# Projections and some MLP passes as two 64-row halves at once, in new engine orders

## The chip, the core and the metric

The kernel runs on one core of a Trainium2 chip. The core has TensorE (PE, the matrix engine, whose weight loads the profile shows apart as PEld), VectorE (DVE), ScalarE (ACT), GpSimd (POOL) and SyncE (SP), which here issues most of the transfers. All five run their own instruction queues in order and wait for each other on semaphores. The metric is the time of one execution on the device in microseconds; lower is better. A time below is a median over runs of one kernel, and the profile is of one execution.

## The reference

With x of 2048 rows and 448 columns (D), the result is a gated sum of two branches:

```
g = sigmoid(x @ gate_w)                      # one gate per row
a = memory_attention(x) @ wo                 # 16 heads of 28, 4 segments of 512 rows
h = layernorm(x)                              # per row
b = (gelu(h.T @ w1 + b1) @ w2 + b2).T         # mixes across the 2048 rows
out = g * a + (1 - g) * b
```

In the attention branch q, k and v are x times a 448x448 matrix each. Within a segment each head does causal softmax attention. It also reads a memory M (28x28) and z (28) that earlier segments have left: `phi(q) M / (phi(q) z + 1e-6)`, with `phi(t) = t + 1` where t > 0, and `exp(t)` elsewhere. Each head mixes the two by `sigmoid(beta)`; then M grows by `phi(k)^T v` and z by the column sums of `phi(k)`. In the other branch the normalised rows are mixed across rows: 2048 to 1792 columns by w1, a bias and a tanh gelu, and back by w2 with a bias.

Both branches read the same x, and all inputs are bf16.

## The kernel before, in words

**How it is put together.** `build_kernel` describes the work as named operations (`op`), each with an engine, a function that emits its instructions, and the tiles it reads and writes. `Sched.plan` then takes the order of each engine's queue from a table of names, `ORDER`, written out in full: `u1-0@6*5` means the operations `u1-0` to `u1-4` in a row, the first of them taking PSUM bank 6. `finalize` gives each operation the semaphore waits it needs. Nothing else sets the order: what stands earlier in an engine's list runs earlier, and waits if it must.

**The names on PE.** `warm` is nine matmuls without use, to keep the array busy at the start; `gtr` turns the gate weights, and DVE's `gw` copies the result into a 449th column of the v weights; `btr` turns the biases. `pr...` and `lo...` are the projections: `t` for v (one per 128 rows, `prt0` to `prt15`), `k` and `q` for one block of 512 rows (0 to 3) and one group of four heads, `x` for a group that holds leftover heads of both k and q. `sc` fills four banks with scores, ACT's `exp` empties them, POOL's `mask` cuts the triangle, `pv` is the product with v, `mem` and `mst` belong to the memory, `wo` and `lw` are the output projection, `u` the first MLP product (14 sums of 16 passes), `y` the second (16 sums of 14; the last in two parts of 320 and 128 columns, the second part named `y15-k#1`).

**The contraction of 448.** 448 is three chunks of 128 and a half. The x chunks start at rows 0, 128, 256 and 320, so that chunk 3 repeats half of chunk 2. `pair(A, B)` computes two projections together, each into its own bank: three full passes of 128 rows each, and one operation `lo` in which A's last 64 rows and B's run as two matmuls in the upper and the lower half of the array. That makes seven passes for two projections. `wo_pair` does likewise for the output projection (`lw` is the shared pass). For the first four v tiles and the first k projections the first chunks are separate operations, `pra` and `prb`.

**Forms of the array.** A matmul uses the array whole, or as row tiles of 64 (`lo`, `lw`) or 32 rows (`sc`), or as column tiles of 32 (`pv`, `mst`), or both (`mem`). `plan` looks at each run of PE operations between row-tiled ones; where a column-tiled one stands in the run, all full passes in it are emitted as four 32-column ones (`mm`, line 282), so that the form does not change within a run.

**Early loads.** On ACT's queue stand, in this order, the loads of v weights chunk 0, gate weights, v weights chunks 1, 2, and the last, then the last k chunk and the biases. On SP's queue stand the two transposing loads of the first 512 rows of x (chunks 0 to 2, chunk 3), k and q weights, then the next rows. DVE copies the k and q weights into a padded layout (`padk`, `padx`, `padq`, line 662) before k and q can run. Normalisation of x for the MLP is DVE work: statistics `bns` (line 916), `bna`, and `ln` (line 932), with a power on POOL in between; `u` passes of row tile t need `ln` of t.

## Time and profile before

| what | value |
|---|---|
| time, median of 3 runs | 170.95 us (170.28 to 175.36) |
| span of the profiled execution, first to last instruction | 168.9 us |
| profiled execution's own time, taken as | 168.9 us, and the 2.05 us by which the median stands above it |
| PE busy | 164.7 us (98%), 2022 matmuls recorded |
| DVE busy | 136.7 us (81%) |
| ACT busy | 130.6 us (77%) |
| POOL busy | 64.3 us (38%) |
| scores, exponential of one fill on ACT | 1.88 us, 40 of them |

How to read the profile: a group of instructions is told by line, engine, operation and tile shape, with its count, its busy time, the mean length of one in ns, and the idle time of the engine before it with what ended that. Most matmuls have line 282, that of the helper `mm`, so shapes tell them apart. A matmul's recorded length holds the time its last columns need to leave the array, so that the lengths of matmuls in a row overlap; the distance of their starts is the pace. The timeline merges like instructions in a row into one line: start, length, work and count. In it a `q` behind an engine's name (ACTq, SPq) means its sequencer, which issues transfers.

### The profile page before, as it was taken

The page shows a single profiled execution, that of the slowest core. Times are in us where ns is not written, and L with a number is a line of the kernel's source. Part 1 is how long each engine was busy: PE and PEld are TensorE (multiplying, and loading weights), DVE is VectorE, ACT ScalarE, POOL GpSimd, SP SyncE. Part 2 cuts the span into 40 slices and gives each one's busy share as a digit, 9 for nine tenths or more (in the row PEclk, how much of TensorE's full clock was granted, in tenths as well). Part 3 has the DMA queues.
Part 4 walks back from the last instruction along what each step waited for, and adds up shares of the span by engine and source line. Part 5 has one row for each costly group of instructions (what it writes and reads, how often), then busy time and mean ns, then how long its engine had stood idle before and what let it go on. Part 6 is the DMA issues. An engine that isn't in the chain of part 4 may idle for free.

```text
span 168.9 us, 4944 instructions
## 1 busy us (share of the span) xinstructions
PE 164.7 (98%) x2022; PEld 78.5 (47%) x2026; DVE 136.7 (81%) x321; ACT 130.6 (77%) x164; POOL 64.3 (38%) x100
## 2 busy tenths in 40 slices
PE   8999999999999999999999999999999999999994
PEld 2334444444554644544453454444454444564553
DVE  0088999877989989999999999999999978695042
ACT  0359999999999997999999998988985788604100
POOL 5000245260442524142177356445837355540000
PEclk9999999999999999999999999999999999999999
DMA  6998999888699945994337302328853129831202
GB/s 144 249 258 289 248 153 246 160 228 226 138 167 254 222 101 146 163 213 124 109 98 169 82 4 65 94 82 111 244 148 110 46 70 280 229 103 60 84 27 82
DMA packets 53974, 25.44 MB, mean 151 GB/s; under 512 B 18416, under 2 KB 53712, under 8 KB 53952
## 3 DMA queue, kind: packets, MB, share of 16 engines
q1 hardware_dynamic: 53160, 24.54, 61.2%
q10 hardware_dynamic: 792, 0.58, 1.7%
q8 instruction: 16, 0.26, 0.7%
q14 instruction: 6, 0.05, 0.1%
HBM read 18.82 MB, written 2.36 MB: 125 GB/s over the span
## 4 chain that ended last, share of the span: by engine, by line
PE 94%; DMA 3%; ACTq 1%; issue 1%; POOL 0%; DVE 0%; POOLq 0%
PE t L282 79%; PE t L973 8%; PE t L1003 5%; DMA t<-in_A_wv_dram 3%; PE t L856 1%; PE t L1076 1%; ACTq L525 1%; ACTq L546 0%; DVE t L1165 0%; POOL t L544 0%; POOL t L620 0%; POOL t L587 0%; POOL t L619 0%; POOL t L615 0%; POOLq L1280 0%
## 5 line engine op out<-in xcount | busy, mean ns | idle before, releaser
L282 PE MATMUL t<-t 128*32 128x448 bf16 (+9 forms) x1257 | 140.4, 352 | 1.0 <-issue 0.6
L282 PEld LDWEIGHTS t<-t 128*32 128x32 bf16 (+2 forms) x1261 | 63.7, 97 | 63.8 <-issue 15.3
L982 ACT ACTIVATE t<-t 128x2048 bf16<-128x2048 f32 x40 | 75.2, 1879 | 6.8 <-PE t L973 6.2
L985 POOL TENSOR_SCALAR_AFFINE_SELECT t<-t 128x512 bf16<-128x512 bf16 x64 | 43.3, 688 | 43.0 <-ACT t L982 40.0
L1040 POOL TENSOR_TENSOR t<-t 128x448 bf16<-128x448 f32 (+2 forms) x13 | 13.3, 1026 | 19.0 <-DVE t L1033 14.4
L1165 DVE SCALAR_TENSOR_TENSOR t<-t 128x448 bf16<-128x448 f32 (+2 forms) x17 | 10.7, 642 | 10.6 <-PE t L282 10.5
L973 PE MATMUL t<-t 28*128 28x512 bf16 (+3 forms) x256 | 15.8, 301 | 0.0
L1017 DVE STREAM_TRANSPOSE t<-t 128x512 f32<-128x512 f32 x16 | 11.3, 706 | 2.9 <-PE t L1003 2.7
L925 POOL TENSOR_TENSOR t<-t 128x4 f32<-128x4 f32 x4 | 4.2, 1054 | 23.4 <-DVE t L923 21.4
L1119 ACT ACTIVATE t<-t 128x448 bf16<-128x448 f32 x10 | 7.1, 732 | 7.6 <-PE t L282 7.6
L1003 PE MATMUL t<-t 128*32 128x512 bf16 (+3 forms) x256 | 11.5, 300 | 0.0
L1059 DVE STREAM_TRANSPOSE t<-t 128x512 bf16<-128x512 bf16 x16 | 10.9, 690 | 0.0
L973 PEld LDWEIGHTS t<-t 28*128 28x128 bf16 x256 | 4.4, 92 | 14.0 <-ACT t L982 7.7
L818 ACT ACTIVATE t<-t 128x448 bf16<-128x448 f32 x13 | 6.8, 546 | 4.2 <-PE t L282 4.2
L916 DVE BATCH_NORM_STATS2 t<-t 128x6 f32<-128x448 bf16 x16 | 9.3, 610 | 0.7 <-DMA t<-in_A_x_dram 0.7
L1145 DVE SCALAR_TENSOR_TENSOR t<-t 128x448 f32<-128x448 f32 x14 | 9.0, 649 | 0.7 <-ACT t L1140 0.6
L1003 PEld LDWEIGHTS t<-t 128*32 128x32 bf16 x256 | 6.7, 96 | 5.3 <-issue 0.7
L1137 ACT ACTIVATE t<-t 128x448 f32<-128x448 f32 x14 | 8.8, 638 | 0.1
L779 ACT ACTIVATE t<-t 128x512 bf16<-128x512 bf16 x12 | 7.6, 635 | 1.4 <-DVE t L736 1.4
L808 DVE SCALAR_TENSOR_TENSOR t<-t 128x512 bf16<-128x512 bf16 x12 | 8.5, 712 | 0.1
L1143 DVE TENSOR_SCALAR t<-t 128x448 f32<-128x448 f32 x10 | 6.5, 676 | 2.4 <-ACT t L1137 2.3
L1033 DVE SCALAR_TENSOR_TENSOR t<-t 128x448 f32<-128x448 f32 x12 | 8.4, 699 | 0.0
(76 smaller groups left out, 132.1 us busy)
## 6 DMA issues: line engine op xcount, KB each, us to landing
t<-in_B_w_dram SPq DMA_DIRECT2D x52, 256.0 KB, 3.9
t<-in_A_x_dram SPq DMA_DIRECT2D x4, 448.0 KB, 5.4
out_dram<-t SPq DMA_DIRECT2D x15, 112.0 KB, 2.0
t<-in_B_w_dram SPq DMA_DIRECT2D x8, 128.0 KB, 2.5
t<-in_A_wv_dram ACTq DMA_DIRECT2D x4, 112.0 KB, 4.1
t<-in_A_wq_dram SPq DMA_DIRECT2D x1, 336.0 KB, 4.8
spare_heads<-t SPq DMA_DIRECT2D x8, 32.0 KB
spare_heads<-t SPq DMA_DIRECT2D x16, 16.0 KB
```

Of the source, the lines that this page charges most:

```text
L282: last = e.matmul(out[q], w[:, q], x, skip_group_check=True, **kw)
L916: op("DVE", lambda e: e.bn_stats(st6[:, t, :], xh[:, t, :]), reads=[R_x[t]], writes=[R_st6[t]], name=f"bns{t}", cost=512, prio=P_PROJ - 10 ...
L973: last = e.matmul(bank(hl)[:, c0 : c0 + w], kT[r, hg, s * 512 + j * 128 : s * 512 + j * 128 + 128], qT[r, hg, s * 512 + 128 * j : s * 512 ...
L982: op("ACT", lambda e: e.activation(pslot(g), ps[:, 0:4, :], ACT.Exp, scale=SCALE), reads=R_bank[0:4], writes=[g.res], take=g, name=f"exp{p ...
L985: op("POOL", lambda e, c0=c0: e.affine_select(pslot(g)[:, :, c0 : c0 + 128], pslot(g)[:, :, c0 : c0 + 128], pattern=[[0, 4], [1, 128]], co ...
L1003: last = e.matmul(bank(cb)[32 * ((hl + hg) % 4) : 32 * ((hl + hg) % 4) + 32, 128 * j : 512], vaug[:, 4 * s + j, 32 * h : 32 * h + 32], psl ...
L1017: dv(lambda e: e.transpose(tt[:, ia, :], bank(cb)[:, 0:512]), [bres(cb)], [R_tt[ia]], "ta", 630, use=(cb,))
L1040: return e.tensor_tensor(dst, part(n3[0]), part(n3[1]), op=ALU.add)
L1059: dv(lambda e: e.transpose(oT[:, hg, s * 512 : s * 512 + 512], o), [R_ob[hg]] + ([R_obx] if hg else []), qres(hg, s), "ot", 635)
L1137: op("ACT", lambda e: e.activation(gg[:, q, :], bank(b)[:, 0:D], ACT.Square, bias=b1s[:, ft : ft + 1], scale=math.sqrt(GC)), **buse(b), re ...
L1145: op("DVE", lambda e: e.scalar_tensor_tensor(gg[:, q, :], gg[:, q, :], 1.0, vh[:, q, :], op0=ALU.add, op1=ALU.mult), reads=[R_gg[q], R_vh[ ...
L1165: op("DVE", lambda e: e.scalar_tensor_tensor(outst[:, p, c0:c1], bank(b)[:, 0 : c1 - c0], omg[:, T : T + 1], ag(T)[:, c0:c1], op0=ALU.mult ...
```

## The change: more pairs as half passes, and all five orders new

`pair` gets a second way, `halves`, used when the PE order asks for it by names (`dt0-0` to `dt0-6` in place of `lot0`, `prt0`, `prt1` and so on). The seven passes of a pair then are seven operations of two 64-row matmuls each: in each, A works on one half of the rows and B on the other half, into their two banks. In the first four A has the upper rows of the array's tile list (rows 0 to 63) and B the others, in the last three it is the other way round. Each operation waits only for the chunk that it reads (`by`). The output projection gets the same (`dw`), and pairs of MLP passes may be split alike (`u10x-2` and `u10y-2`: first one half for one sum with the other half for the other sum, then the halves change sides).

A half pass that writes a bank in which the other 64 rows wrote last now waits for that earlier operation on PE's own semaphore (`rows`, `wrote`). `btr` uses 64 rows instead of 128. The y sums no longer wait for all gelu results at their first pass, only each pass for its own. All five orders are new; 116 passes are in half form by the new names (v tiles 0 to 5, 10 and 11; k of blocks 0 and 2 in part; q of block 0 and the split third group of block 1; output tiles 6, 7, 10, 11; five row tiles of `u10`/`u11`, nine of `u12`/`u13`, two of `y8`/`y9`), of which the old form had 12 already as `lo` or `lw`. ACT's early loads are reordered, and some copies out of PSUM move between ACT and DVE.

```
+        wrote = {}
+        for o in self.per_eng["PE"]:
+            for b, k in o.rows:
+                mine = wrote.setdefault(b.bank if isinstance(b, Bank) else b, {})
+                o.deps = o.deps + ([mine[1 - k]] if 1 - k in mine else [])
+                mine[k] = o
...
+    def twice(name, sides, needs, bs, take, n, prio, tops, **kw):
+
+        def fn(e):
+            for (w, x), b, sm in zip(sides, bs, take):
+                last = mm(e, bank(b)[:, 0:n], w, x, **sm.flags())
+            return last
...
+    def halves(A, B, bs, prio):
+        sums = [Sum(7), Sum(7)]
+        for i, sides in enumerate((((0, 0), (0, 1)), ((1, 0), (1, 1)), ((2, 0), (2, 1)), ((3, 0), (3, 1)), ((0, 1), (0, 0)),
+                                   ((1, 1), (1, 0)), ((3, 1), (2, 0)))):
+            rows = [slice(64 * k, 64 * k + 64) for c, k in sides]
+            twice(f"d{A['name'][2:]}-{i}", [(P["w"](c, r), P["x"](c, r)) for P, (c, k), r in zip((A, B), sides, rows)],
+                  [r for P, (c, k) in zip((A, B), sides) for r in P["by"](c)], bs, sums, A["n"], prio, [k for c, k in sides],
+                  use=A["use"])
+        for P, b in zip((A, B), bs):
+            P["out"](b)
...
+                 by=lambda c: [rx[c // 3], R_wv[c], R_gw],
...
+    def both(stem, first, n, nk, bs, w, x, need, prio):
+        twin = [k for k in range(nk) if f"{stem}{first}x-{k}" in asked]
+        sums = [Sum(nk + len(twin)) for _ in bs]
+        for k in range(nk):
+            if k in twin:
+                for xy in range(2):
+                    rows = [slice(64 * h, 64 * h + 64) for h in (xy, 1 - xy)]
+                    twice(f"{stem}{first}{'xy'[xy]}-{k}", [(w(i, k, r), x(k, r)) for i, r in enumerate(rows)], need(k), bs, sums,
+                          n, prio, (xy, 1 - xy))
+                continue
...
 ORDER = {
     "PE": """
-warm gtr@4 warm2 pra0@7 pra1@4 pra2@5 pra3@6 prb3 prb2 prb0 prb1 lot2 lot0 prt1 prt3 prt2 prt0 pra0_1 pra0_2 pra0_0
-btr@7 lok0_0 lok0_2 prk0_0 prx0_3 prk0_2 prk0_1 prt7@4 prx1_3@5 prk1_2@6 lot6@7 lok1_2 loq0_0 loq0_2 prq0_2 prq0_0
...
+warm gtr@4 warm2 dt0-5@56 dt2-5@74 dt0-1 dt2-2 dt2-1 dt0-2 dt0-0 dt2-6 dt2-4 dt0-3 dt2-0 dt2-3 dt0-6 dk0_0-0*4 dt0-4
+dk0_0-4 dk0_2-0*2 dk0_0-5 dk0_2-2*2 dk0_0-6 dk0_2-4*2 lot6@67 lok1_2@45 dk0_2-6 prt6 prt7 prx1_3 prk1_2 prq1_1@6
+prq1_0@7 dq0_2-0*2 loq1_0 dq1_2-3@54 dq1_2-1 dq0_2-2 dq1_2-0 dq1_2-2 dq0_0-0 dq1_2-5 btr@6 dq0_0-1 dq1_2-6 dq0_0-2
...
     "ACT": """
-ldwv0 ldgw ldwv1 ldwv2 ldwvb ldwkb ldb1 ldb2 cpv2 cpv0 gt0 gt2 cpv1 gt3 gt1 ek0_0 cpk0_1 cpk0_3 cpq0_3 ek0_1 cpv7
...
+ldwvb ldwv2 ldwv1 ldwv0 ldgw ldwkb cpv3 cpv1 ldb1 gt1 gt2 gt3 ldb2 gt0 cpk0_2 cpv6 cpq0_3 cpv7 gt6 gt7 cpk1_3 cpq1_3
```

More of the change, by code (lines that the diff above doesn't have):

```diff
@@ L44 @@
                  "cost", "lat", "prio", "mode", "start", "end", "pos", "nbytes", "alts", "rel", "port", "take",
-                 "free", "hold", "tile", "cols")
+                 "free", "hold", "tile", "cols", "rows")
 class Sum:
@@ L706, in pair @@
            take=bs if isinstance(bs[0], Bank) and "first" not in A else None, name="lo" + A["name"][2:], mode="h",
-           cost=pe_cost(max(A["n"], B["n"])) + 4, prio=prio, hold=wait, adds=free)
+           cost=pe_cost(max(A["n"], B["n"])) + 4, prio=prio, hold=wait, adds=free, rows=((bs[0], 1), (bs[1], 0)))
         for (P, b, cs, c, rows), sm in zip(parts, sums):
@@ L1225, in build_kernel @@
     do_mst(2)
-    mlp = [(mm1, ft) for ft in range(NFT)] + [(mm2, T) for T in range(NT - 1)] + [(mm2_last, NT - 1)]
     for u in range(16):
```

269 lines of the change are left out of this document (161 added, 108 removed).

## The prediction

> **What bounds the kernel now.** The page was read first: busy shares and the chain of waits.
>
> ```profile
> span 168.9 us, 4944 instructions
> ...
> PE 164.7 (98%) x2022; PEld 78.5 (47%) x2026; DVE 136.7 (81%) x321; ACT 130.6 (77%) x164; POOL 64.3 (38%) x100
> ...
> PE 94%; DMA 3%; ACTq 1%; issue 1%; POOL 0%; DVE 0%; POOLq 0%
> ```
>
> TensorE (PE) carries 94% of the chain. Then the busy times by stage (columns: stretch, its length, busy time and count of PE, of the weight loads PEld, of DVE, ACT, POOL, then clock, DMA share, GB/s):
>
> ```profile
> 8.95:20.70 11.75, 11.70 (x67) 5.28 (x68) 10.43 (x32) 10.11 (x27) 1.04 (x1) 1.00 1.03 260
> 20.70:104.20 83.50, 82.87 (x1113) 39.48 (x1116) 77.07 (x193) 80.54 (x104) 34.93 (x49) 1.00 0.70 153
> 104.20:146.20 42.00, 42.00 (x593) 19.50 (x596) 37.70 (x75) 35.25 (x30) 22.53 (x31) 1.00 0.54 139
> ```
>
> From 8.95 us on PE has next to no gap, so a microsecond taken off PE's queue, or added to it, comes out at the end. The exceptions are in PE's timeline at the start (start, length, work; idle time and its releaser in brackets):
>
> ```profile
> 0.82 4.00 PE L651 MATMUL t<-const-bfloat16-1.0 128*128 128x512 bf16 x9 [0.82 <-PEq L1280]
> 4.62 0.21 PE L839 MATMUL t<-t 128*128 128x3 bf16 x1
> ...
> 5.21 2.02 PE L282 MATMUL t<-t 128*128 128x449 bf16 x8
> 7.52 2.90 PE L282 MATMUL t<-t 64*128 64x449 bf16 x14 [0.29 <-DMA t<-in_A_wv_dram]
> ...
> 23.51 0.40 PE L973 MATMUL t<-t 28*128 28x384 bf16 x8
> 24.16 2.64 PE L282 MATMUL t<-t 128*128 128x512 bf16 x13 [0.26 <-issue]
> ```
>
> Warm-up to 4.6; `gtr` (L839, which turns the gate weights) at 4.62; the first eight v passes at 5.21; a wait for the v weights before 7.52. The k projection's first pass starts at 8.95 (where I cut the stages). PE waits once more before 24.16.
>
> **The change, part by part.** The array's work does not change: a pair had six full passes and one pass of two 64-row halves, and has seven passes of two halves. By my count in the two orders 104 full passes become half pairs, while 128-row columns streamed stay the same in sum. What can change is the cost of a pass, the changes of tile form, waits, and when the stream starts.
>
> *A pass of two halves.* Before has some in a row:
>
> ```profile
> 14.17 0.58 PE L282 MATMUL t<-t 64*128 64x449 bf16 x4
> ...
> 14.37 0.59 PE L282 MATMUL t<-t 64*128 64x512 bf16 x4
> ...
> 14.59 0.49 PE L282 MATMUL t<-t 64*128 64x512 bf16 x4
> ```
>
> Their starts are 0.20 and 0.22 us apart (these are three answers for short windows), each for two matmuls, of 449 and 512 columns: the two halves run at once, at 0.43 ns a column, as the full passes below do (0.19 for 448). So 104 passes cost 0. The page "TensorE: Matmul & The Clock Gate" of the Trainium skill (part 3, what overlaps) speaks against the change: a weight load overlaps running matmuls only where the row group differs, and in a run of half pairs both row groups are always busy. What it would make of the time stands as a rival, worked out from a row.
>
> *Changes of tile form.* Around two score groups, late in the kernel (PE, then ACT):
>
> ```profile
> 118.81 0.39 PE L973 MATMUL t<-t 28*128 28x512 bf16 x4
> 119.14 2.07 PE L282 MATMUL t<-t 128*128 128x448 bf16 x10
> 121.19 0.40 PE L973 MATMUL t<-t 28*128 28x384 bf16 x8
> ...
> 119.26 1.88 ACT L982 ACTIVATE t<-t 128x2048 bf16<-128x2048 f32 x1
> 121.03 0.72 ACT L1119 ACTIVATE t<-t 128x448 bf16<-128x448 f32 x1
> 121.64 1.88 ACT L982 ACTIVATE t<-t 128x2048 bf16<-128x2048 f32 x1
> ```
>
> The first score group streams 512 columns (0.22 us at the pace of the half pairs) and the next form starts 0.33 us after it: a change of form costs 0.11. Counting forms (full, 64-row, 32-column, scores, memory) along the two orders gives 114 changes before and 106 after, of which 2 and 1 lie ahead of the first k pass: 7 fewer behind it, 7 x 0.11 = **-0.77 us**. A change costs the same in each kind, so I give it no wider bounds than 0.09 to 0.13 (-0.6 to -0.9).
>
> *Score groups that wait for the exponential.* The same rows: ten passes of 0.19 and one change are 2.00 us, but 119.14 to 121.19 is 2.05. The exponential ended at 121.14 (119.26 + 1.88) and the scores, which overwrite its banks, started 0.05 later. From score to score that loop takes 0.45 + 1.88 + 0.05 = 2.38 us. In the old order, between fill 3 of pair 4 and the last fill, six stretches hold only ten full passes (2.33) and wait 0.05 each, and one waits 0.06 for ACT; in the new one the shortest holds 2.44. **-0.36 us**, at best -0.4, at worst 0 (if ACT slips).
>
> *Self waits.* New: a half pass that writes a bank with the other 64 rows than the pass before waits on PE's own semaphore. Behind the waiting instruction PE's whole queue stands, and all evacuations of those banks.
>
> ```profile
> L282 PE MATMUL t<-t 128*128 128x448 bf16 x319 | 66.1, 353 | 0.0
> L282 PE MATMUL t<-t 128*32 128x448 bf16 x652 | 35.9, 353 | 0.0
> L282 PEld LDWEIGHTS t<-t 64*128 64x128 bf16 x64 | 2.6, 93 | 7.2 <-issue 4.5 <-DMA t<-in_A_x_dram 0.7 <-ACT t L821 0.5
> ```
>
> A pass of 448 is recorded 0.353 long but frees the array after 0.19, so it completes about 0.16 after its columns. In the new order eight half passes have just one other pass between themselves and the one they wait for (`dt0-1`, `dt2-0`, `dk0_0-4`, `dk0_2-4`, `dq1_2-5`, `dt4-0`, `dk2_2-4`, `u10y-10`); all others have two or more and 0.2 us to spare. Each of the eight waits 0.16 + 0.05 (the hop seen above) - 0.19 = 0.03 to 0.04. Bounds: 0, and a whole change of form, 0.11. Six lie behind the first k pass: **+0.24** (0 to +0.66).
>
> *32-column passes.* 181 before, 224 after by count. Busy time a pass is 35.9 / 163 = 0.220 against 66.1 / 319 = 0.207; the difference is the tail that closes each short run. I take 0; as an upper bound 43 x 0.013 = +0.6.
>
> *The start.* All v weights' loads and the small gate load stand on ACT's queue, and the change reorders it: the gate load moves from second place to fifth.
>
> ```profile
> 0.79 0.38 ACTq L525 DMA_DIRECT2D t<-in_A_wv_dram  x1
> 1.21 0.75 ACTq L546 DMA_DIRECT2D t<-in_gate_w_dram  x1
> 1.99 0.94 ACTq L525 DMA_DIRECT2D t<-in_A_wv_dram  x2
> 2.96 0.60 ACTq L529 DMA_DIRECT2D t<-in_A_wv_dram  x1
> ...
> t<-in_A_wv_dram ACTq DMA_DIRECT2D x4, 112.0 KB, 4.1
> ```
>
> Every v pass reads the gate column, which `gtr` and one DVE copy make from that load: 4.62 to 5.21, 0.59 us. The load's issue moves from 1.21 to 0.79 + 0.38 + 0.94 + 0.60, about 2.75, behind 448 KB on its own queue. Bounds: it lands before the warm-up ends (4.6), or as late as the last v piece did (7.4, just ahead of 7.52). With the 4.1 us of the wv loads it would be 6.85; the queue no longer stands still for the 0.75 us issue, so I take **6.5**. First v pass then at 7.1. Thirteen of the fourteen v passes come before the first k pass (13 x 0.19, and two self waits): 9.64. On the other side the k passes cannot start before the padded weights:
>
> ```profile
> 8.43 0.47 DVE L662 COPY t<-t 128x784 bf16<-128x784 bf16 x2 [3.36 <-DMA t<-in_A_wk_dram]
> ...
> 9.34 0.81 DVE L662 COPY t<-t 128x392 bf16<-128x392 bf16 x6
> ```
>
> These free the first k pass at 8.9, in both kernels. So the k stage starts 9.64 - 8.95 = 0.69 later, with one v pass (0.19) still to do: **+0.88 us** (+0.19 if the gate load lands by 5.8, +1.8 if at 7.4). The old wait before 7.52 saves nothing, the padding hid it.
>
> *The wait before 24.16.* From 23.51 the scores stream 512 columns (0.22) and one change (0.11) follows; 0.32 is left over, which the row puts to no releaser. The old order runs `prk2_1` there, which needs both parts of the third x transpose. The new one starts that stage with chunks of the first part and reaches the second part 0.7 us later: **-0.32** (0 at worst).
>
> *Other moves, each at nothing.* `btr` takes 64 rows, with no change of form around it. Evacuations that go from ACT to DVE or back are hidden while PE has a filled queue; cover gone, they cost what the DVE rival says. The SP queue's order after 24 us (W1 pieces, gathers, WO) is moved past by a few places; loads land 2.5 to 5 us after issue, and the order of the u passes has moved with them. At the end twelve y passes of 128 columns stand behind the last 320-column one instead of fourteen:
>
> ```profile
> 163.75 2.76 PE L282 MATMUL t<-t 128*128 128x448 bf16 x27
> ...
> 165.77 0.55 DVE L1165 SCALAR_TENSOR_TENSOR t<-t 128x320 bf16<-128x320 f32 x1 [0.95 <-PE t L282]
> 166.55 0.35 DVE L1165 SCALAR_TENSOR_TENSOR t<-t 128x128 bf16<-128x128 f32 x1 [0.23 <-PE t L282]
> ```
>
> DVE has 0.23 to spare before its last piece, and the two passes fewer (0.06 each) use half of it: the end stays 0.35 behind PE's. `ag14` and `ag15` now run on DVE ahead of `fin14`:
>
> ```profile
> L1123 DVE TENSOR_SCALAR t<-t 128x448 bf16<-128x448 f32 x6 | 4.4, 733 | 0.6 <-PE t L282 0.5
> ```
>
> From `wo15` to the last 320-column pass PE has seven of those, two full and two short y passes, 1.5 us by their columns, and DVE one `ag` and one `fin` (0.73 + 0.68): just covered; without the cover, about 0.1 us.
>
> **Sum.** 0.88 - 0.77 + 0.24 - 0.36 - 0.32 = -0.33 us. The profiled execution: 168.9 - 0.33 = 168.57. The median of the runs shown, 170.95, is 2.05 above that span (launch and end, untouched): 168.57 + 2.05 = **170.6 us**.
>
> **Rivals.**
> *A, the gate load is early.* The gate load is only 1.5 KB; if it slips through by 5.8, the k stage starts on the pads as before: 0.69 less. With self waits at 0 another 0.24: 170.6 - 0.9 = 169.7. For it: on the old queue it was in by the end of the warm-up. Against it: 448 KB ahead on the same queue.
>
> *B, slower: the late gate load leaves the array cold.* Nine warm-up passes take 4.00 us, 0.43 each, twice the 0.22 of a 512-column pass. The eight passes from 5.21 take 2.02, less the last one's 0.16 tail 1.86, where 8 x 0.19 is 1.51: about two of them ran at half pace, so the array came to full speed at about 5.9, with PE busy throughout. In the new order PE has nothing from 4.6 to 6.5. If the full pace then comes only after a new busy stretch, the thirteen v passes go at 0.38: 13 x 0.19 = +2.5, 173.1 us; with the load at 7.4, 174.0. It decides once the gate load lands after the warm-up and before the array has been granted full speed. The same page (part 1) has the clock rise after a busy window of about 3.4 us and fall after an idle one as long: by that rule a gap of 1.9 us costs nothing once the clock is up, and it would be up or not by where the free-running window lies; the 5.9 here agrees with a rise in the second window.
>
> *C, DVE is late with the normalised x.*
>
> ```profile
> L916 DVE BATCH_NORM_STATS2 t<-t 128x6 f32<-128x448 bf16 x16 | 9.3, 610 | 0.7 <-DMA t<-in_A_x_dram 0.7
> ...
> L932 DVE TENSOR_SCALAR t<-t 128x448 bf16<-128x448 bf16 x16 | 5.6, 389 | 0.0
> ```
>
> The new order starts the first MLP passes out of row order; `u0-9` is the eleventh. Ahead of its x tile DVE has, after the three k copies (ending at about 14.9), 15 statistics (8.7), 8 normalisations (2.8) and some 3.3 of aggregates, copies and small work (my estimate): 14.9 + 14.8 = 29.7. PE reaches `u0-9` at 29.8 by my count. A DVE chain 10% longer would hold PE 1.5 us, of which little comes back: 172.1.
>
> *D, weight loads show, or halves don't overlap.* By the skill's rule above each added pass would expose a load: 104 x 0.093 (the 64x128 row) = +9.7, 180.3 us. The starts 0.20 and 0.22 apart with two loads each say no.
>
> **How the numbers follow.** Forecast as summed 0.60; A 0.16; B 0.13; C 0.08; D 0.02; something not seen 0.01. The forecast's own range is 169.9 (gate load by 5.8) to 171.9 (load at 7.4, self waits 0.1 each). Leaving out the dear half of B, of C and all of D, and the best of A, the range is 169.3 to 173.0. A measurement of this kernel tells about 2% from no change, 167.5 and 174.4 us: nothing summed here reaches 167.5 (0.03); above 174.4 lie D and the joint ends of B and C (0.06); within, 0.91.
>
> **What would show it.** `gtr` in PE's timeline should start near 6.5 (A: 4.6; B: v passes 0.38 apart), the first 64-row 512 pass near 9.6, with its predecessors 0.19 apart; runs of half pairs at 0.19 and 0.215; no PE gap before the first MLP passes (C: gaps released by L932); scores 2.44 or more apart late on. The prediction is wrong if half pairs are spaced by more than 0.25, if PE's stream from the first k pass is not about 1.2 us shorter than before (157.6 us from 8.95 to PE's end at 166.5), or if PE shows gaps in the middle.

## The result, and the profile after

The changed kernel takes **179.17 us** (median of 4 runs, 177.98 to 179.71), the kernel before 170.75 beside it: a ratio of 1.049 (95% interval 1.044 to 1.054). It is 8.4 us slower, where the prediction had -0.3. One of the four executions of the kernel before (175.36) was over 1.5% slower than its fastest and is left out of the ratio. The page of the profile (span, busy times, chain of waits):

```profile
span 176.8 us, 5428 instructions
...
PE 166.6 (94%) x2259; PEld 77.6 (44%) x2259; DVE 148.9 (84%) x341; ACT 126.6 (72%) x154; POOL 57.5 (33%) x90
...
PE 69%; DVE 17%; DMA 7%; ACT 2%; ACTq 1%; issue 1%; SPq 1%
```

PE's busy time has hardly moved (164.7 to 166.6), the span has grown by 7.9. The chain tells it more sharply: PE carried 94% of it before and carries 69% now, DVE has gone from nothing to 17% and transfers from 3% to 7%. DVE is busy for 12 us more (136.7 to 148.9).

Busy times by stage (columns as in the prediction). The cuts are the first v pass, the first scores `sc0_0`, `sc5_0`, `sc7_4` and PE's end:

```profile
8.41:26.18 17.77, 17.77 (x146) 7.65 (x145) 13.88 (x47) 10.89 (x29) 1.63 (x5) 0.93 1.14 240
26.18:114.50 88.32, 84.97 (x1232) 39.17 (x1232) 82.61 (x195) 81.31 (x100) 35.54 (x45) 1.00 0.56 136
114.50:156.00 41.50, 41.13 (x614) 19.25 (x607) 37.57 (x75) 30.57 (x25) 16.70 (x26) 1.00 0.48 134
```

In the stage from 26 to 114 us PE has 3.35 us of gaps; before, the same stage (20.77 to 106.70) had 0.63. Some shorter waits lie inside the busy time, since a matmul's record holds its tail. The granted clock is below 1 in the first row. That row's cause is seen in PE's timeline (start, length, work, idle time before it and its releaser) and in the page's line on the v weights' transfers:

```profile
0.82 3.67 PE L679 MATMUL t<-const-bfloat16-1.0 128*128 128x512 bf16 x9 [0.82 <-PEq L1375]
7.82 0.19 PE L894 MATMUL t<-t 128*128 128x3 bf16 x1 [3.33 <-DMA t<-in_gate_w_dram]
...
8.41 6.95 PE L296 MATMUL t<-t 64*128 64x449 bf16 x54
```

```profile
t<-in_A_wv_dram ACTq DMA_DIRECT2D x4, 112.0 KB, 4.6
```

`gtr` starts at 7.82, when the gate load behind the four v pieces lands; PE had stood still for 3.33 us. Stretches of 3.4 us of the same seconds, with the granted clock in the third column from the right:

```profile
4.00:7.40 3.40, 0.49 (x2) 0.00 (x0) 0.00 (x0) 1.28 (x1) 0.00 (x0) 1.00 1.22 225
7.40:10.80 3.40, 2.98 (x17) 1.04 (x19) 1.45 (x9) 0.00 (x0) 0.00 (x0) 0.50 1.18 322
10.80:14.20 3.40, 3.40 (x36) 1.40 (x32) 1.56 (x4) 1.32 (x5) 0.00 (x0) 0.99 1.02 269
```

The array was at full clock from 4.0 on, stood still, and was granted half the clock from 7.4 to 10.8, just when the v passes ran. PE's waits behind that (what waited on what: us in total, times, longest):

```profile
PE t L894 <- DMA t<-in_gate_w_dram: 3.3, 1, 3.3
PE t L911 <- DMA t<-t: 1.2, 1, 1.2
PE t L1028 <- DVE t L1139: 0.9, 1, 0.9
PE t L679 <- PEq L1375: 0.8, 1, 0.8
PE t L296 <- DVE t L1229: 0.5, 2, 0.3
```

These are new but for the fourth: `mst1` (L911) waits for a transposing transfer, the scores `sc2_3` (L1028) for DVE's copies of the memory product (L1139). The chain of waits between 60 and 84 us shows how full DVE is there (pieces in order of time: start, length, what):

```profile
62.70 0.54 DVE t L1236
63.23 0.60 DVE t L837
63.83 1.04 DVE t L862
64.87 0.59 DVE t L1229
...
67.70 0.97 DVE t L1236
68.67 1.23 DVE t L1139 x2
...
69.96 1.22 DVE t L1139 x2
...
71.23 0.40 PE t L1028 x4
...
77.66 4.45 DMA t<-t
...
82.15 0.66 PE t L911 x64
```

The ledger, read from the trace as the start of the first matmul of each step (us):

| kernel | first v pass | first k pass | `sc0_0` | `sc5_0` | `sc7_4` | PE's end | k pass to end |
|---|---|---|---|---|---|---|---|
| before | 5.21 | 8.95 | 20.77 | 106.70 | 143.86 | 166.51 | 157.6 |
| after | 8.41 | 12.13 | 26.18 | 114.50 | 155.99 | 174.41 | 162.3 |

So 3.2 us are lost ahead of the first k pass and 4.7 behind it. The new order does other work between the same marks: with the prices of the prediction (0.19 and 0.22 a pass, 0.11 a change of form, 2.38 a score loop) and no other wait it should need about 156.5 from the first k pass to the end, against 157.6 for the old one. By these prices, which no run measured one by one, the queue's waits are about 5.8 us.

### The profile page after: what moved, and what is told of

The parts are those of the page before. It is cut to its first block, busy times and chain, and to the rows that moved or that the text cites. A ratio compares the mean times of both kernels' runs of the same rounds, so it can differ in the third digit from the quotient of the medians.

```text
span 176.8 us, 5428 instructions
## 1 busy us (share of the span) xinstructions
PE 166.6 (94%) x2259; PEld 77.6 (44%) x2259; DVE 148.9 (84%) x341; ACT 126.6 (72%) x154; POOL 57.5 (33%) x90
## 4 chain that ended last, share of the span: by engine, by line
PE 69%; DVE 17%; DMA 7%; ACT 2%; ACTq 1%; issue 1%; SPq 1%
PE t L296 58%; PE t L1028 5%; PE t L1058 4%; DVE t L1236 3%; DVE t L1139 3%; DMA t<-in_gate_w_dram 3%; DMA t<-t 3%; DVE t L837 2%; DMA t<-spare_heads 2%; DVE t L862 2%; DVE t L1229 2%; DVE t L1231 1%; ACT t L1037 1%; ACTq L553 1%; PE t L911 1%; DVE t L1072 1%
## 5 line engine op out<-in xcount | busy, mean ns | idle before, releaser
L296 PE MATMUL t<-t 128*32 128x448 bf16 (+9 forms) x1494 | 142.6, 354 | 1.3 <-DVE t L1229 0.5
L296 PEld LDWEIGHTS t<-t 128*32 128x32 bf16 (+2 forms) x1494 | 62.9, 97 | 66.9 <-issue 17.3
L1040 POOL TENSOR_SCALAR_AFFINE_SELECT t<-t 128x512 bf16<-128x512 bf16 x64 | 44.8, 716 | 52.2 <-ACT t L1037 51.1
L1028 PE MATMUL t<-t 28*128 28x512 bf16 (+3 forms) x256 | 15.9, 301 | 1.2 <-DVE t L1139 0.9
L1095 POOL TENSOR_TENSOR t<-t 128x448 bf16<-128x448 f32 (+1 forms) x5 | 6.3, 1258 | 22.0 <-DVE t L1088 11.9
L1172 DVE TENSOR_SCALAR t<-t 128x448 bf16<-128x448 f32 x11 | 8.1, 738 | 6.0 <-PE t L296 5.8
L872 ACT ACTIVATE t<-t 128x448 bf16<-128x448 f32 x11 | 6.0, 547 | 8.6 <-PE t L296 8.5
L1028 PEld LDWEIGHTS t<-t 28*128 28x128 bf16 x256 | 4.5, 92 | 15.1 <-ACT t L1037 7.1
L1229 DVE TENSOR_SCALAR t<-t 128x448 f32<-128x448 f32 x12 | 8.0, 673 | 3.4 <-ACT t L1223 3.2
L1236 DVE SCALAR_TENSOR_TENSOR t<-t 128x448 bf16<-128x448 f32 x14 | 10.1, 736 | 0.0
L1168 ACT ACTIVATE t<-t 128x448 bf16<-128x448 f32 x5 | 3.6, 724 | 8.2 <-PE t L296 8.2
L862 DVE SCALAR_TENSOR_TENSOR t<-t 128x512 bf16<-128x512 bf16 x12 | 9.2, 767 | 0.0
L837 DVE SCALAR_TENSOR_TENSOR t<-t 128x512 bf16<-128x512 bf16 x12 | 9.1, 756 | 0.0
```

What stands on the lines that cost most here:

```text
L296: last = e.matmul(out[q], w[:, q], x, skip_group_check=True, **kw)
L837: op("DVE", lambda e: e.scalar_tensor_tensor(kphi[:, p, :], ks, 0.0, kphi[:, p, :], op0=ALU.max, op1=ALU.add), reads=kres(hg, tc) + [R_kph ...
L862: op("DVE", lambda e: e.scalar_tensor_tensor(ph, qs, 0.0, ph, op0=ALU.max, op1=ALU.add), reads=qres(hg, tc) + [R_phq[hg][tc]], writes=[R_p ...
L1028: last = e.matmul(bank(hl)[:, c0 : c0 + w], kT[r, hg, s * 512 + j * 128 : s * 512 + j * 128 + 128], qT[r, hg, s * 512 + 128 * j : s * 512 ...
L1040: op("POOL", lambda e, c0=c0: e.affine_select(pslot(g)[:, :, c0 : c0 + 128], pslot(g)[:, :, c0 : c0 + 128], pattern=[[0, 4], [1, 128]], co ...
L1229: alt=("DVE", lambda e: e.tensor_scalar(vh[:, q, :], bank(b)[:, 0:D], 0.5, b1h[:, ft : ft + 1], op0=ALU.mult, op1=ALU.add), dve_cost(448)))
```

## Experiments

Theory S at first: two separate losses, the late gate load at the start, and waits in the middle where PE waits for DVE, ACT and transfers in the new orders. (All five orders are new, and no run here takes PE's order apart from the others.) Rivals: M, that the middle's waits follow from the late start; H, that the half form itself costs. The kernels are compared by their medians; each interval is that of the ratio to the kernel before.

### 1. Where the start goes

**Gate load second on ACT's queue.**

```
-ldwvb ldwv2 ldwv1 ldwv0 ldgw ldwkb
+ldwvb ldgw ldwv2 ldwv1 ldwv0 ldwkb
```

> The changed kernel with one word moved: the gate weights' load goes from fifth back to second place on ACT's queue. Theory S (start): the late gate load costs what it delays the first k pass, 12.1 to about 9.0 us, and the half clock from 7.4 to 10.8 us is part of that; the middle keeps its own waits: 179.2 - 3.1 = 176 us. Rival M (the waits in the middle are only a consequence of the late start): they go too, 170 to 172 us. If the start were absorbed by later waits anyway: 178 to 179 us.

Measured: 178.26 us (1.045, 1.042 to 1.049). `gtr` starts at 4.08, but PE then waits 2.54 us for v chunk 1, which the new PE order reads first and which is third in this queue. The first v pass is at 7.04, the first k pass at 11.17 with the clock halved from 6.9 to 10.3: 1.0 us gained at the start, of which most is lost again at `sc7_2`, where the wait for the gathered heads has grown from 0.3 to 1.1. So this run didn't mend the start, and M is still open.

**The same late gate load in the kernel before.**

```
-ldwv0 ldgw ldwv1 ldwv2 ldwvb ldwkb
+ldwv0 ldwv1 ldwv2 ldwvb ldgw ldwkb
```

> The kernel before with the gate weights' load moved from second to fifth place on ACT's queue, all else as before. Theory S: PE has nothing from 4.6 to about 7.8 us, its clock falls back, and the first k pass moves from 8.95 to 11.5 or 12: 170.75 + 2.5 to 3.1 = 173.3 to 173.9 us, with no new waits in the middle. Rival M: waits in the middle appear as they did in the changed kernel, 176 us or more.

Measured: 174.82 us (1.026, 1.021 to 1.030). PE's timeline:

```profile
8.04 0.18 PE L839 MATMUL t<-t 128*128 128x3 bf16 x1 [3.21 <-DMA t<-in_gate_w_dram]
...
8.61 6.19 PE L282 MATMUL t<-t 128*128 128x449 bf16 x22
```

One word in one queue costs the old kernel 4.2 us; the time is 0.9 more than the dearer end of what was expected of it. Its first k pass is at 13.34 (8.95 before). Its v passes run 0.37 apart until 12.6 us and 0.19 after (the profile has no record of the clock before 12.6 and shows 1.00 there, so the pace has to tell), so here the clock came up late, where in the changed kernel it had been up and fell. From the k pass on PE's stream is that of before (157.3 us to its end, 157.6 before), with no new wait in the middle. In the old orders a late start alone does not make the middle's waits, which speaks against M.

**A longer warm-up in the changed kernel.**

```
-warm_up(9, "warm", -1)
+warm_up(22, "warm", -1)
```

> The changed kernel with 22 warm-up passes instead of 9, which keep PE busy until about the time when the gate load lands; nothing else is changed. Theory S: the clock stays up, the first v passes run 0.19 apart instead of 0.37, and the first k pass comes at about 10.8 instead of 12.1 us: 1.0 to 1.3 us less, 178 us, if the waits of the middle are not what absorbs it. If the idle time alone counts and not the clock: 179 us.

Measured: 177.28 us (1.038, 1.034 to 1.042). The gate load is as late as ever, but PE is busy until it lands:

```profile
0.82 7.59 PE L679 MATMUL t<-const-bfloat16-1.0 128*128 128x512 bf16 x22 [0.82 <-PEq L1375]
8.26 0.17 PE L894 MATMUL t<-t 128*128 128x3 bf16 x1
```

The clock stays up. From the first v pass (8.81) to the first k pass (11.48) it takes 2.67 us, 0.19 a pass, where the changed kernel takes 3.72. The clock's fall is a loss of its own, on top of the late load.

**The queue in the order in which the new PE order reads.**

```
-ldwvb ldwv2 ldwv1 ldwv0 ldgw ldwkb
+ldwv1 ldgw ldwv2 ldwv0 ldwvb ldwkb
```

> The changed kernel with ACT's early loads in the order in which its first passes need them: v chunk 1, gate weights, v chunks 2, 0 and the last. Theory S + D: v passes from 5.2 us on, no long gap, the clock stays up, first k pass at 9.0 to 9.5 instead of 12.1; the waits of the middle (0.96, 0.38, 1.36 and 0.68 us) stay: 179.2 - 2.8 = 176.4 us. Rival M: they go too, 170 to 172. Rival G (a late gather of k absorbs part at the score group of 150 us, as with the gate load alone): 177 us.

Measured: 175.41 us (1.028, 1.026 to 1.030), 1.0 less than theory S had; the first k pass is at 8.80, before the old kernel's. The start is worth 3.8 us by the medians, 3.3 by the first k pass of the two traces (12.13 to 8.80), and is mended. 4.8 us over the kernel before are left, and from the first k pass to PE's end it takes 162.4, as in the changed kernel: M, which had 170 to 172, falls.

### 2. Is it the half form?

**The changed kernel with whole passes** (its orders; each pair back as three full passes and one `lo`).

```
-dt0-5@56 dt2-5@74 dt0-1 dt2-2 dt2-1 dt0-2 ...
+pra0@5 pra2@7 pra1@6 pra3@4 prb2 prb0 prb1 prb3 lot2 lot0 ...
```

> The changed kernel with every half-pass operation undone in place: the twelve pairs, the MLP chunks and all else stand at the same places of the new orders, but as full passes and one shared pass. By count 127 changes of tile form instead of 106, the same columns. Theory H (a half pair costs what a full pass costs, and self waits next to nothing): +21 x 0.11 = +2.3 us on PE, less what the waits of the middle absorb: 180.5 to 181.5 us. Rival (the half form itself costs, by weight loads or self waits): the time falls, 176 us or less.

Measured: 180.16 us (1.056, 1.052 to 1.060). This is 1.0 more than the changed kernel, 0.3 below the range expected. In its trace the start is 0.75 later (first k pass at 12.88); from there to PE's end it takes 162.4, in the changed kernel 162.3. So the 2.3 worked out for 21 more changes of form don't show as such. Waits are gone in their place (`mst1`'s 1.2 and the gather's 0.3 are 1.5 of it), and the price of a change is not measured apart. Taking the half passes away takes nothing off the loss.

**Half passes in the old orders** (v tiles 0 to 5, 10, 11, k of block 0, output tiles 6 and 7).

```
-pra0@7 pra1@4 pra2@5 pra3@6 prb3 prb2 prb0 prb1 lot2 lot0 prt1 prt3 prt2 prt0 pra0_1 pra0_2 pra0_0 btr@7 ...
+dt0-0@74 dt2-0@56 dt0-4 dt2-4 dt0-5 dt2-5 ... dk0_0-0*2 dk0_2-0*2 dk0_0-2 btr@7 ...
...
-lw6@45 y5-7 pv10@7 wo7
+dw6-0@45*7 y5-7 pv10@7
```

> The new code with the kernel before's five orders, in which only pairs of the change become half passes at the places that they had: v tiles 0 to 3, the k projections of block 0, v tiles 4 and 5, 10 and 11, output tiles 6 and 7 (half-form passes 32 before, 74.5 here, 136.5 in the changed kernel). Form changes 112 by count, 114 before. If the half form itself cost the middle's 4.8 us (0.046 for each of 104 more passes), the 42 more passes here would cost 2.0: 172.7. If the form costs nothing and the loss is in the orders: 170.75 less two changes (0.2), within 0.5: 170.0 to 171.1.

Measured: 173.11 us (1.015, 1.012 to 1.018), by its number a point for H. The trace names other causes: 0.8 us of waiting for the padded weights (the half passes were put in an order that needs them sooner, and the evacuation `cpv3` held them back on DVE), three runs of seven adjacent half passes that wait 0.23 each where the halves change sides, and 0.4 for an exponential.

**The same for the start alone, those causes avoided.** A first try (v tiles 0 to 3 and k of block 0, `cpv3` behind the pads):

> The new code with the kernel before's orders; only v tiles 0 to 3 and the k projections of block 0 become half passes (24 full passes become half pairs), with at least two passes between the two halves of a bank where possible, and the copy cpv3 moved behind the padded k weights on DVE (in the earlier run of this kind it held the pads back, 1.0 us, and three runs of seven adjacent half passes waited 0.23 each). Form changes 112, before 114. If half passes cost nothing: 170.75 less 0.2, within 0.3. If they cost 0.06 a pair: 172.

Measured: 171.55 (1.005, 1.003 to 1.007): the pads still held PE 1.0 us, since the pair with the leftover heads needs two padded q weights more. With that pair behind the other:

```
-dk0_0-0 dk0_2-0 dk0_0-1 dk0_2-1 dk0_0-2 btr@7 ...
+dk0_0-0*4 btr@7 dk0_2-0*2 dk0_0-4 dk0_2-2*2 dk0_0-5*2 dk0_2-4*3
```

> The new code with the kernel before's orders and half passes for v tiles 0 to 3 and k of block 0 alone, as in the earlier run (171.55), but the pair with the leftover heads, which needs two more padded weights, stands behind the first four half passes of the other pair, and cpv3 stands behind all six pads and the first two of q. If half passes cost nothing by themselves, the 1.0 us wait for the pads goes: 170.4 to 170.8, the level of the kernel before. If they do cost: 171 or more with no such wait in the trace.

Measured: 171.13 us (1.0027, 1.0016 to 1.0038), above the level expected. Where the 0.3 are:

```profile
PE t L296 <- DVE t L690: 1.2, 2, 1.0
```

This still waits for the pads (L690); the k weights landed about 0.5 later than in the kernel before. From `sc0_0` to `sc7_4` it takes 122.8, before 123.1. The change's other code (`btr` in 64 rows, the y sums' own waits) runs here too, so it costs nothing visible there. And in the changed kernel itself four half pairs in a row read

```profile
13.44 1.03 PE L296 MATMUL t<-t 64*128 64x512 bf16 x8
```

which, less the 0.37 us that the last one is recorded, is (1.03 - 0.37) / 3 = 0.22 from pair to pair, as for full passes. H falls: neither run makes the half form the loss. Apart from the 0.23 where a pair changes sides with nothing between, what half passes cost here is indirect: both projections of a pair run side by side and so need the later one's inputs.

### 3. What the middle waits for

**Ten additions back from DVE to POOL**, alone and together with the gate load second.

```
 "DVE": -oy0 -ox0 -ox4 -ox8 -o9 -o10 -oy12 -ox12 -o14 -o15
 "POOL": +oy0 +ox0 +ox4 +ox8 +o9 +o10 +oy12 +ox12 +o14 +o15
```

> The changed kernel with the ten output additions and copies (oy0, ox0, ox4, ox8, o9, o10, oy12, ox12, o14, o15) that it moved from POOL to DVE put back on POOL, the start left late. Theory D (DVE is overfull between 58 and 110 us and PE waits for it): some 5 us of DVE work less, of which 1.5 us lie before 110 us: PE's waits in the middle shrink by 1 to 2 us, 177 to 178 us. Rival M: no change, 179 us. Rival: POOL's slower additions hold the output projection, 180 us.

> Both edits of the two single ones: gate load second and the ten additions on POOL. Theories S and D add up: 174 to 175 us. Rival M: as the gate load alone, 170 to 172 us.

Measured: 180.86 (1.059, 1.056 to 1.062) and 179.29 (1.052, 1.049 to 1.055): slower than the changed kernel, or no faster. In the first the start itself came later (the wait for the gate load is 4.0 us, the first k pass at 13.69), and from there to PE's end it takes 163.3, in the changed kernel 162.3. `mst1`'s wait goes, `sc2_3`'s 0.9 stays, and the product with v now waits 0.8 for POOL's masks. But this did not test a lighter DVE. Ten operations fewer, some 5 us, left DVE as busy as it was (148.9 us):

```profile
PE 167.9 (94%) x2256; PEld 77.4 (43%) x2259; DVE 148.4 (83%) x331; ACT 126.4 (70%) x154; POOL 66.2 (37%) x100
```

Other operations of DVE became longer: one step of phi of k, for example, has a mean of 788 ns where the changed kernel has 692. POOL was busier meanwhile, 66.2 us instead of 57.5. Section 4 shows DVE's operations lengthened by POOL's masks; that POOL's additions did it here was not run apart.

**Nine operations off DVE ahead of the waits** (three additions to POOL, six evacuations to ACT).

> The changed kernel, start left late, with nine operations that it had moved to DVE and that stand ahead of 110 us put back: oy0, ox0, ox4 on POOL, gvh1, gvh3, gvh9, gvh10, cpv9, cpv11 on ACT; some 5.5 us less on DVE. Theory D (DVE's backlog makes PE wait in the middle): the waits at the memory's copies and at the second memory sum, 0.96 and 1.36 us, and those of 0.3 to 0.5 behind them shrink by 2 to 3 us in all: 176.5 us. Rival: ACT, which gets 3.8 us of it, holds the scores instead and it is no gain, 179 us or more.

Measured: 179.71 (1.054, 1.048 to 1.059). `sc2_3`'s wait is the same 0.9, ACT now holds scores (0.6) and the gather's wait is 1.1. Here too some 5.5 us were to leave DVE and 1.7 did:

```profile
PE 166.5 (94%) x2259; PEld 77.4 (44%) x2259; DVE 147.2 (83%) x332; ACT 129.2 (73%) x160; POOL 60.3 (34%) x93
```

So moving these operations buys nothing. What it buys when DVE really is busy for less is seen only in section 4.

**One step in DVE's order** (on top of the mended start): the memory copies `tm` ahead, the third phi of k earlier, the last gather ahead of three stores on SP.

```
-ot1 garg7 gelu6 tm7 tm6 eps7 tm5 tm4
+ot1 tm7 tm6 eps7 tm5 tm4 garg7 gelu6
...
-phk1_3 ot2 ta4 ta3 garg8 phk1_2
+phk1_3 phk1_2 ot2 ta4 ta3 garg8
...
-gk3_h0 out5 out4 out6 ldw2_6_2 gk3_h1 ldw2_6_0
+gk3_h0 gk3_h1 out5 out4 out6 ldw2_6_2 ldw2_6_0
```

> The changed kernel with the start mended (175.41) and three moves in the orders alone, no operation changes its engine: on DVE the four copies of the memory product stand ahead of one evacuation and one gelu (they were behind them), the third phi of k of block 1 stands six places earlier, and on SP the last gather of block 3 stands ahead of three output stores. Theory O (each of the middle's waits comes from the place of one operation in one queue): the wait of 0.96 ahead of the scores sc2_3 goes to under 0.1, that of 0.45 ahead of the memory sum mst1 goes, and nothing comes back, so 173.5 to 174.2. Theory F (DVE has no room at all between 26 and 106 us, so any operation moved ahead makes another one late): the waits named go, others of the same sum appear behind them, and the time stays at 175.0 to 175.8.

Measured: 176.61 (1.035, 1.032 to 1.038), 1.2 slower than without. `sc2_3`'s wait is gone, `mst1`'s and `sc7_2`'s too. In their place, on ACT and then on PE, and in the stretches between the clock's records, which stand 3.41 us apart (clock third from the right):

```profile
67.23 0.58 ACT L1234 ACTIVATE t<-t 128x448 f32<-128x448 f32 x1 [2.60 <-DVE t L1231]
```

```profile
72.23 0.40 PE L1028 MATMUL t<-t 28*128 28x384 bf16 x8 [2.45 <-ACT t L1037]
```

```profile
70.09:73.50 3.41, 1.27 (x33) 0.71 (x36) 3.41 (x8) 3.41 (x4) 0.00 (x0) 1.00 0.03 8
73.50:76.91 3.41, 3.41 (x40) 1.31 (x32) 3.41 (x7) 2.16 (x3) 2.22 (x3) 0.50 0.30 66
```

`garg7` (L1231, on which ACT's tanh L1234 waits), moved behind the copies, let ACT stand 2.6 us; everything behind it on ACT, the exponential too, was late; PE waited 2.45; and the clock then fell to half for 3.4 us, 1.7 more. Neither theory had this number. F (no room on DVE) fits it better than O, though part of it is the clock, which neither had.

**`garg7` ahead of the copies again.**

> The moves of the run with the reordered DVE and SP queues, but the four copies of the memory product now stand behind the evacuation garg7 (ACT's gelu step waited 2.6 us for it when it stood behind them) and ahead of gelu6 alone. Theory O (places in the queues): sc2_3's wait of 0.96 goes to at most 0.1, mst1's 0.45 goes, the scores sc7_2 wait no longer for the gather; 175.41 - 1.3 to 2.1 = 173.3 to 174.1. Theory F (DVE has no room): again another wait in their place, 175.0 or more.

Measured: 176.49 (1.034, 1.032 to 1.037). (`garg7` is the argument of a tanh, not an evacuation as I called it.) `sc2_3` waits 0.3 and `sc7_2` no longer; but `mst1` waits 1.6, for the transposing transfer `tk1_2`, which was issued no later than with the mended start alone (74.68, there 75.01) and took 4.65 us to land instead of 2.97. By its expectation O fails again.

**That transfer earlier on SP as well.**

```
-tk1_3 ldwo1b go0_0 ldwl11 gq2_2 tk1_2
+tk1_3 tk1_2 ldwo1b go0_0 ldwl11 gq2_2
```

> The second reordering (176.49) and one move more: on SP the transposing load tk1_2, for which the memory sum mst1 waited 1.6 us there, stands directly behind tk1_3, ahead of four other issues (2.5 us of issuing). Theory O (single places in the queues): it lands some 2.5 us sooner, mst1's wait goes, 176.49 - 1.6 = 174.9, and if the waits mended so far don't come back elsewhere, down to 173.8. Theory F: other waits take its place, 175.5 or more.

Measured: 174.04 (1.021, 1.018 to 1.024). SP's issues of the changed kernel and of this one:

```profile
73.84 1.20 SPq L840 DMA_TRANSPOSE t<-t  x1
75.09 0.56 SPq L624 DMA_DIRECT2D t<-in_A_wo_dram  x1
75.70 0.67 SPq L1118 DMA_DIRECT2D t<-t  x1
76.42 0.59 SPq L624 DMA_DIRECT2D t<-in_A_wo_dram  x1
77.05 0.56 SPq L814 DMA_DIRECT2D spare_heads<-t  x1
77.66 1.22 SPq L840 DMA_TRANSPOSE t<-t  x1
```

```profile
70.30 2.51 SPq L840 DMA_TRANSPOSE t<-t  x2
```

The second transpose needs no waiting for four other issues, lands 2.5 us after its issue (74.00; PE needs it at 77), and `mst1` does not wait. 1.4 us are won against the mended start, 5.1 against the changed kernel. From `sc0_0` to `sc7_4` it takes 127.7 (before 123.1, the new order's own work 124.2). What is left are one wait of 0.8 among the first v passes and about ten of 0.2 to 0.5 us.

### 4. DVE and POOL at once

DVE's operations of one shape are not equally long. POOL's masks and DVE's long pieces in the changed kernel:

```profile
63.22 2.15 POOL L1040 TENSOR_SCALAR_AFFINE_SELECT t<-t 128x512 bf16<-128x512 bf16 x2 [2.25 <-ACT t L1037]
66.59 2.57 POOL L1040 TENSOR_SCALAR_AFFINE_SELECT t<-t 128x512 bf16<-128x512 bf16 x3 [1.23 <-ACT t L1037]
```

```profile
63.75 1.12 DVE L862 SCALAR_TENSOR_TENSOR t<-t 128x512 bf16<-128x512 bf16 x1
...
65.59 0.68 DVE L862 SCALAR_TENSOR_TENSOR t<-t 128x512 bf16<-128x512 bf16 x1
```

The same operation takes 1.12 us beside the masks that run from 63.22 to 65.37, and 0.68 in the gap behind them. A kernel without masks shows what that is worth; it would also take away PE's own waits for masks, but the changed kernel's list of waits above has none.

```
-        for x, j, c0, w in FILLS[f]:
+        for x, j, c0, w in ():
             op("POOL", lambda e, c0=c0: e.affine_select(...
```

> The changed kernel with the start mended (175.41), with POOL's 64 causal masks left out: the scores above the diagonal stay in, so a part of the computation is missing. DVE has the same work and the same order. Theory C (the middle's 4.8 us come from DVE operations that run longer while a POOL mask runs, 7 us of excess by the trace, 5 more than before): without masks DVE's busy time falls by 4 to 6 us, sc2_3's wait of 0.96 falls to about 0.1, the sum of the middle's waits falls below 2, 172 to 173. Theory O (order): DVE's busy time falls alike, but the waits stay above 3.5, 174.2 to 175.

> The kernel before with POOL's 64 causal masks left out, the control for the run before. Its DVE shows 2 us of such excess and its PE hardly waits in the middle. Theory C: DVE's busy time falls by about 2, PE's end moves by less than 0.5, 170.2 to 170.8. If the masks themselves held the product with v (their own time, not DVE's), this kernel would gain as much as the changed one does.

Measured: 173.27 us (171.21 to 174.72; 1.012, 1.004 to 1.020) with the mended start, 170.54 (1.000, 0.9985 to 1.0014) for the old kernel. Two groups of DVE, with masks (mended start) and without:

```profile
L1236 DVE SCALAR_TENSOR_TENSOR t<-t 128x448 bf16<-128x448 f32 x14 | 10.1, 738 | 0.0
...
L862 DVE SCALAR_TENSOR_TENSOR t<-t 128x512 bf16<-128x512 bf16 x12 | 9.2, 767 | 0.0
```

```profile
L1236 DVE SCALAR_TENSOR_TENSOR t<-t 128x448 bf16<-128x448 f32 x14 | 8.4, 616 | 0.2 <-ACT t L1234 0.2
...
L862 DVE SCALAR_TENSOR_TENSOR t<-t 128x512 bf16<-128x512 bf16 x12 | 8.1, 675 | 0.0
```

DVE's busy time falls from 148.3 to 141.9, 6.4 us, in the new orders and from 136.7 to 134.3, 2.4 us, in the old ones: the new orders put more of DVE's two-input work beside masks (the old kernel's like group had a mean of 615 with masks). The Trainium skill, page "GPSIMD Engine Reference" (1. Specifications), says that GpSimd's SBUF interfaces are shared with VectorE and that instructions with two SBUF inputs contend; that agrees, and the number is the 738 against 616 ns above. Of the 12 us that DVE is busier after the change than before, 7.6 remain without masks (141.9 against 134.3); the other 4 are operations made longer. Of the 6.4 us 2.1 come out at the end by the medians; the two intervals allow about 1 to 4. That lies between the two theories, nearer C: DVE's time and `sc2_3`'s wait went as C had it, the other waits did not. In the old kernel nothing comes out; its PE's list of waits has none for DVE.

The profiled execution without masks was the longest of its four (174.72), with 1.3 us for `tk1_2` and 1.4 for the gather; hence the runs with those mended as well. First with the DVE and SP moves of experiment 3:

> The same with the 64 causal masks left out (a part of the computation is missing). Without masks alone the kernel took 173.27, and its trace still had PE wait 1.3 us for a transposing DMA that stands behind the third phi of k of block 1, and 1.4 us for the gather on SP; both stand earlier here. If collisions on DVE and these two places are the whole of the middle's loss, 170.4 to 171.2, PE's waits between sc0_0 and sc7_4 under 1.5. If ACT's lateness (0.9 ahead of sc1_2) and others are a third part, 171.5 to 172.5.

Measured: 174.51 (1.022, 1.017 to 1.027), 2.0 above the higher of the two ranges. The four executions spread from 173.20 to 175.72, and the profiled one is the longest. In it `tk1_2` took 4.57 us to land here too, PE stood for 1.85 us, and the clock fell once more (cut at the clock's records again):

```profile
76.57:79.98 3.41, 1.56 (x89) 0.86 (x85) 1.26 (x3) 3.19 (x6) 0.00 (x0) 1.00 0.50 111
79.98:83.39 3.41, 3.41 (x44) 1.86 (x40) 2.33 (x6) 1.09 (x3) 1.05 (x1) 0.50 0.59 161
```

Then with `tk1_2` early:

> The same with the 64 causal masks left out (a part of the computation is missing). The run like it without the move took 174.51; its PE waited 2.0 us at mst1, and the granted clock then stood at about 0.5 for some 3.4 us, 1.7 us more. If collisions with masks and the two transfers are the rest of the middle's loss: both go, 174.51 - 3.7 = 170.8 (170.4 to 171.6). If other queue places are left that cost over 1 us: 172 or more.

Measured: 173.15 us (172.07 to 174.55; 1.014, 1.009 to 1.020), beside 174.04 with masks. The two transfers' waits are gone and DVE's in the middle too; a new one is there, and the clock stays up across it:

```profile
PE t L296 <- ACT t L1168: 1.9, 1, 1.9
```

```profile
103.76:107.17 3.41, 2.22 (x18) 1.33 (x22) 1.77 (x7) 3.33 (x4) 0.00 (x0) 1.00 0.00 0
```

That is `loq3_2`, whose bank an evacuation on ACT (L1168) frees late. By the expectation this is the case of other queue places that still cost. So the named places and the masks together are not the whole of it: about 2.4 us over the kernel before remain, and each mended place has let another come forward.

## Why the prediction was wrong, step by step

- **The start** (+0.88, "I take 6.5"): mis-sized, and beyond its own upper bound. `gtr` started at 7.82, so the gate load landed at about 7.8, not by 7.4. The four v pieces took 4.6 us where I had argued with 4.1, and the small load landed after all of them. The first v pass came 1.3 us later than I had it, at 8.41.
- **Rival B's mechanism** (chance 0.13) held: the v passes ran at half pace. I had the clock come up late, as it did in the old kernel with the late load; here it was up and fell again. The Trainium skill's rule that I weighed there, page "TensorE: Matmul & The Clock Gate" (Part 1), has the clock fall after an idle window of about 3.4 us. Here PE stood for 3.33 us, and in the stretch ahead of the fall it was at work for 0.49 of 3.40; in two later kernels waits of 2.45 and 1.85 us were enough. That is less than the rule asks for, and the measurement decides: a gap of 1.9 us, which by the rule costs nothing, can cost a stretch at half clock, as 1.85 did. Late load and half clock together are 2.5 us at the first k pass (12.13 for 9.64), and mending the queue's order gave 3.8 in the median.
- **"Other moves, each at nothing"** failed, and is the larger error: with the start mended, 4.8 us over the kernel before remain, and PE's waits there are for DVE, ACT and transfers. I had called the cover a "filled queue" on PE. But a full queue in order hides nothing when its head waits. The rows that I quoted held the warning: DVE was busy for 77.1 of 83.5 us in the middle before the change, and the change makes DVE busy for 12 us more, 7.6 of them moved work. I checked it at one place, `u0-9`, where it held, instead of at every place where PE takes a bank back.
- **Rival C** (DVE late, 0.08) had the engine right, the place and the price wrong: no wait of weight at the first MLP passes, but 0.9 at `sc2_3` and 0.2 to 0.3 each at three other places where PE waits for DVE (L1229, L1236).
- **Form changes, score loops and the wait before 24.16** (-0.77, -0.36, -0.32): nothing here contradicts them as PE's own work (106 changes are in the trace, and no wait is listed at those places), but no run measured the price of a change apart. By those prices the stream from the first k pass is about 156.5, 1.1 shorter than before; I had 1.2. It was measured at 162.3, since waits of about 5.8 stand in it.
- **Half passes at 0** held: 0.22 apart in the trace, and the old kernel with half passes at the start keeps its later stages (122.8, before 123.1). **Rival D** (weight loads show, 180.3) has a number close to the result by chance and no row for it: with whole passes the kernel is 1.0 slower still.
- **Self waits at 0.03 to 0.04**: about that in the trace. Where the halves change sides without a pass between them, 0.23 was measured.
- **The range** (169.3 to 173.0) left out what the text had priced at nothing. Its ends were made of the steps that I had costed.

What stays open: of the 4.8 us of the middle, four moves in the orders, two on DVE and two on SP, gave 1.4, and leaving out the masks about 2 (0.9 on top of those moves, with wide intervals). The rest, some 2.4 to 3.3 us, is many short waits that change places from kernel to kernel; I could not settle it on one cause, nor on one of the five queues. Why `tk1_2` landed in 2.4 to 3.6 us in some runs and 4.4 to 4.7 in others was not tried. No version here beats the kernel before.

## What to carry to other kernels

A reordered queue is priced by its tightest meeting points, not by its length: for each transfer or evacuation that is moved, find who waits for it and how much slack is left, `tk1_2` had 23 us before and none after. Put the smallest load that everything needs ahead of the large ones on its queue, and keep the array busy until it lands. Orders that are packed to the last tenth of a microsecond pay for each stretched operation and each slow landing.

## What the runs showed of the hardware

- PE's clock fell to half after less than 3.4 us without work. Its records stand 3.41 us apart. Waits of 3.33, 2.45 and 1.85 us (at the start, in the reordered kernel, in the one without masks) were each followed by one such stretch at 0.50, in which a pass of 0.19 takes 0.37. What tells these waits from others is PE's idle time within one stretch: 2.94, 2.14 and 1.85 us of the 3.41 ahead of the falls. The wait of 1.9 in the last kernel without masks lies across two stretches, with 1.19 us idle in the first (2.22 busy in the row above), and the clock stayed up; so it did in every trace here after a stretch with 1.2 us idle or less. In these traces the limit thus lies between 1.2 and 1.85 us of 3.41.
- The small gate load, fifth on its queue behind four pieces of 112 KB, landed at about 7.8 us (`gtr` starts at 7.82); second on it, it was in by 4.1 (`gtr` at 4.08).
- Single VectorE operations with two tensor inputs took 1.04 to 1.12 us beside a GpSimd mask, and 0.68 in a gap between masks; without masks the means fell from 738 to 616 ns and from 767 to 675.
- One transposing transfer, the same bytes, landed 2.4 us after its issue in the kernel before and 4.45 in the changed one.
